# One decoding step of attention with an MLP: the query's copy released at a head's last maximum, and the closing weighted sums split anew

## The chip, the cores and the metric

The kernel runs on one core of a Trainium2 chip. The metric is the device time of one execution in microseconds (us). A core has five engines with queues of their own: TensorE (PE in a profile; its weight loads are PEld), VectorE (DVE), ScalarE (ACT), GpSimd (POOL) and SyncE (SP), which issues the transfers here. An engine takes its queue in order; between engines only semaphores order the work.

## The reference

One token x of 512 numbers is normalized and goes through grouped-query attention over a cache and through an MLP; both results are added to x.

```
xn = layernorm(x)                                  # 512
q  = (xn @ wq)                                     # 32 query heads of 128, 8 key/value heads
scores = q . k_cache * 128**-0.5                   # k_cache, v_cache: 8 heads x 65536 keys x 128
o  = softmax(scores) @ v_cache
y  = x + o.reshape(4096) @ wo + relu(xn @ w1) @ w2 # w1: 512 x 1792, w2: 1792 x 512
```

All is fp32. The two caches are 537 MB of the 561 MB that are read.

## The kernel before

**Opening.** SyncE loads wq in two transfers into the V buffer, then w1, then the first K part. GpSimd fills constants (`flip`, `ident`, `accq`, `qall`, `accy`). VectorE computes the layernorm (L214 to L245) and multiplies the 32 slices of wq by x's numbers in a hardware loop (L256 to L261). TensorE folds that into q (L264). VectorE then builds small constants: `blk` (L269), which TensorE needs for the normalized x (L284); `idg` (L282, L283); later `sel` (L326 to L328), `selb`, `selg` and `rowg` (L333). The MLP's first product (w1) and the relu end in `hs[:, :14]`, the 14 scales of w2's slices.

**Main loop.** Each of the 8 heads has 4 parts of 16384 keys; a step is one part. K and V of a part are 8 MB each. There is one K buffer and one V buffer, so SyncE issues V of step i when V's buffer is free and K of step i+1 when K's is. In a step TensorE makes scores (L380) from the query in `qcur`, VectorE transposes them (L436) and takes maxima (L445, L450), ScalarE exponentiates (L416), and TensorE sums over V (L398) into `acc_o`. At the end of a head VectorE scales and sums `masked` (L479, L484) and adds `kept` (L486).

**The query's copy.** GpSimd holds all queries in `qall` and copies the next head's into `qcur` (L411) when `f_out` is raised (waited for at L410). VectorE raises `f_out` at L484. The copy is made after the last head too, of an empty column.

**Closing sums.** 14 slices of w2 and 32 of wo remain, each 128 x 512 numbers (256 KB), each to be scaled by its column of `hs` and summed over partitions and slices. Arrived slices lie one behind the other in the old K buffer. They are loaded in pieces: w2 as 3, 4 and 7 slices and wo as 9, 7, 5, 4, 4, 1, 1 and 1 (the list `WO`). w2 and wo's first two wait for the K buffer (`k_free`), the rest for the V buffer (`v_free`). In a profile's table of transfers w1 and w2 are `w`. The slices are worked off in four ways:

- The first `FIRST` = 7, all w2: ScalarE scales in place (L500), GpSimd adds into `accy` (L501).
- The next 2 x `TURNS` = 32, in a hardware loop of 16 turns (L532): in each, ScalarE scales the even slice (L538) and TensorE sums it with ones into `acc_z` (L540), while VectorE multiplies the odd slice and adds it into `accy` (L543).
- wo's slices from there to `DIRECT` = 29: TensorE alone, the scale as weights, one slice per column group of `acc_z` (L547).
- The last three: TensorE into `acc_y` (L559).

VectorE folds `accy` and `acc_z` (L554), TensorE sums that into `acc_y` (L559), VectorE transposes it (L583) and SyncE stores 2 KB.

The loop's turns are handed out by GpSimd: for each piece that arrives it raises `go_dve` (L528) and `go_act` (L529) by the slices in it. These instructions stand behind the seven adds in GpSimd's queue:

```
for j in range(FIRST):
    begun = kv[:, j * D : (j + 1) * D]
    AC.op(lambda e: e.activation(begun, begun, AF.Copy, scale=hs[:, j : j + 1]), w2_in[j])
    GP.op(lambda e: e.tensor_add(accy, accy, begun), AC.mark, GP.mark)
...
    ge.wait_ge(*arrivals[at]).then_inc(go_dve, sum((j - FIRST) % 2 for j in js))
    ge.sem_inc(go_act, sum((j - FIRST) % 2 == 0 for j in js))
```

The scales of wo's slices come from VectorE: the reciprocal of the softmax sums (L490, L492, L497), the heads' outputs spread by TensorE (L506) and transposed (L510), and their product (L512). GpSimd hands out wo's slices only behind L512, and VectorE enters the loop only behind GpSimd's last add.

Of the kernel before, what the change touches and what calls it, by code (L numbers as in the profile page):

```python
# [11 lines left out]
AX = mybir.AxisListType  # L12
# [3 lines left out]
P = 128  # L16
# [4 lines left out]
G = HQ // HKV  # L21
CT = 4
# [7 lines left out]
NP = NCH  # L30
STEPS = HKV * NP
WIDE = 4
A = D // P
FB = DFF // P
R = HKV
SLICES = R * G
WO = [9, 7, 5, 4, 4, 1, 1, 1]
DIRECT = 29
LATE = 21 * D
TURNS = 16  # L40
FIRST = 7
EPS = 1e-5


# [26 lines left out]
def attention_and_mlp_kernel(  # L71
# [30 lines left out]
    te, ve, se, ge, sy = nc.tensor, nc.vector, nc.scalar, nc.gpsimd, nc.sync  # L102
# [9 lines left out]
    t1, t2 = place("t1", A * DFF), ks[:, : FB * D]  # L112
# [6 lines left out]
    x16, xc, sq, xn16 = (place(n, 32, rows=R * 2) for n in ("x16", "xc", "sq", "xn16"))  # L119
    xw, xn = place("xw", R, A), place("xn", A)  # L120
    rep, blk = (place(n, P, rows=R * 2) for n in ("rep", "blk"))
# [7 lines left out]
    ident, ones = place("ident", P), place("ones", P)  # L129
    sel, selb, selg = place("sel", WIDE, G), place("selb", WIDE), place("selg", G)  # L130
    rowg = place("rowg", P, rows=G)
    idg = place("idg", G + 1, rows=G)
    qall, qcur = place("qall", HKV + 1, G), place("qcur", 32)
    m, mc = place("m", G), place("mc", G)
    mg = place("mg", 1, rows=G)
# [15 lines left out]
    pr, pt, pz = pa[:, 0, :], pb[:, 0, :], pb[:, 1, :]  # L151
# [16 lines left out]
    def load_slices(name, dst, src, counts, at=0):  # L168
        marks = []
        for n in counts:  # L170
            cut = slice((at + len(marks)) * D, (at + len(marks) + n) * D)
            marks += [load(sy, f"{name}{at + len(marks)}", dst[:, cut], src[:, cut])] * n
        return marks
# [14 lines left out]
    def memset(flow, ap, value):  # L188
        return flow.op(lambda e: e.memset(ap, value))

    far_dve, far_act, far_pool = (e.mark_branch_hint_location() for e in (ve, se, ge))
    memset(GP, flip, 0.0)
    flat_free = GP.mark
    g0 = memset(GP, ident, 0.0)
# [9 lines left out]
    memset(GP, qall, 0.0)  # L204
    memset(GP, accy, 0.0)
    blank = GP.mark
    memset(DV, ones, 1.0)
    memset(DV, qcur, 0.0)
    memset(DV, pm, 0.0)


    half = R * 2
    DV.op(
        lambda e: e.tensor_copy(  # L214
            rep.rearrange("i (h j) -> i h j", j=half), ident[:half, :half].unsqueeze(1).to_broadcast([half, HKV, half])
# [40 lines left out]
    with nc.Fori(0, SLICES, engines=[ENG.DVE]) as t:  # L256
# [8 lines left out]


    spread_x = masked[:half].rearrange("i b d -> i (b d)")
    DV.op(
        lambda e: e.tensor_copy(  # L269
            blk.rearrange("i (j r) -> i j r", r=R), ident[:half, :half].unsqueeze(2).to_broadcast([half, half, R])  # L270
        )
    )
    blk_in = DV.mark
    DV.op(lambda e: e.reduce_sum(eighth, ident.rearrange("p (i r) -> p r i", r=R), axis=AX.X))
    DV.op(
        lambda e: e.tensor_mul(
# [2 lines left out]
        ),  # L279
    )  # L280
    x_spread = DV.mark
    DV.op(lambda e: e.memset(idg, 1.0))  # L282
    DV.op(lambda e: e.tensor_copy(idg[:, :G], ident[:G, :G]), DV.mark)  # L283
    xn_in = PE.op(lambda e: e.matmul(pz[:, :32], blk, xn16, start=True, stop=True), blk_in)  # L284
    DV.op(lambda e: e.tensor_copy(rows[:HKV], pr[:HKV]), q_in_rows)
    for g in range(G):
        PE.op(
# [1 line left out]
            DV.mark,  # L289
        )  # L290
    q_turned = PE.mark
    PE.op(lambda e: e.matmul(acc_z, ident[:half], spread_x, start=True, stop=False), x_spread)
    DV.op(
        lambda e: e.tensor_mul(
            xw, x_of.rearrange("p (r a) -> p r a", a=A), eighth.unsqueeze(2).to_broadcast([P, R, A])
        ),
        xn_in,
    )
    DV.op(lambda e: e.reduce_sum(xn, xw.rearrange("p r a -> p a r"), axis=AX.X), DV.mark)
    DV.op(  # L300
# [14 lines left out]
    for c in range(CT):  # L315
# [4 lines left out]
    mlp_in = PE.mark  # L320


    places = [ident[:, 32 * c : 32 * c + WIDE * G].rearrange("p (b g) -> p b g", g=G) for c in range(CT)]
    memset(DV, acc_o, 0.0)
    memset(DV, acc_y[:, :P], 0.0)
    DV.op(lambda e: e.tensor_add(sel, places[0], places[1]), made)  # L326
    DV.op(lambda e: e.tensor_add(sel, sel, places[2]), DV.mark)
    DV.op(lambda e: e.tensor_add(sel, sel, places[3]), DV.mark)  # L328
    s = DV.mark
    DV.op(lambda e: e.reduce_sum(selb, sel, axis=AX.X), s)  # L330
    DV.op(lambda e: e.reduce_sum(selg, sel.rearrange("p b g -> p g b"), axis=AX.X), s)
    DV.op(
        lambda e: e.tensor_copy(  # L333
            rowg.rearrange("g (i j) -> g i j", j=G), ident[:G, :G].unsqueeze(1).to_broadcast([G, P // G, G])
        )
    )
    DV.op(lambda e: e.transpose(turned, pm[:, : 32 * FB]), mlp_in)
    DV.op(
        lambda e: e.tensor_scalar_max(hs[:, :FB], turned.rearrange("p (j l) -> p j l", l=32)[:, :, 0], 0.0), DV.mark
# [19 lines left out]
    sy.dma_start(vs[:, :LATE], v_parts[STEPS - 1][:, :LATE]).then_inc(v_in, 16)  # L359
    sy.dma_start(vs[:, LATE:], v_parts[STEPS - 1][:, LATE:]).then_inc(v_late, 16)  # L360
    sy.wait_ge(k_free, 1)
    w2_in = load_slices("w2", t2, w2.rearrange("p j n -> p (j n)"), [3, FB // 2 - 3, FB // 2])
    wo_of = wo.rearrange("h (i r) g f -> (h i) (r g f)", r=R)
    near = [n for i, n in enumerate(WO) if FB + sum(WO[: i + 1]) <= SLICES]
    wo_in = load_slices("wo", wos, wo_of, near)
# [41 lines left out]
    with nc.Fori(0, HKV, engines=[ENG.DVE, ENG.Activation, ENG.Pool]) as h:  # L407
        fin_d, fin_s = finss[:, bass.ds(h * (DH + G), DH)], finss[:, bass.ds(h * (DH + G) + DH, G)]
        ve.lower_ap(fin_d), ve.lower_ap(fin_s)
        ge.wait_ge(f_out, 1).then_inc(f_out, -1)  # L410
        ge.tensor_copy(qcur[:, :G], qalls[:, bass.ds((h + 1) * G, G)]).then_inc(q_in, NP)  # L411

        for n in range(NP):
            se.wait_ge(s_bias, 1).then_inc(s_bias, -1)  # L414
            for g in range(G):
                i = se.activation(  # L416
                    wt[:, :, g], tr[:, :, g], AF.Exp, bias=bias[:, n, g : g + 1],
                    scale=scale, accum_out=part[:, n, g : g + 1],
                )
            i.then_inc(s_w, 1)  # L420
            if n:
                se.activation(
                    alpha[:, n : n + 1], bias[:, n - 1, G : G + 1], AF.Exp,
                    bias=bias[:, n, G : G + 1], scale=-1.0,
                ).then_inc(s_alpha, 1)
        se.wait_ge(s_diff, 1).then_inc(s_diff, -1)
        se.activation(
            fac.rearrange("p n g -> p (n g)"), diff.rearrange("p n g -> p (n g)"), AF.Exp
        ).then_inc(s_alpha, 1)

        for n in range(NP):
            for s in range(0, NT, 2):
                if s == NT - 2:

                    ve.wait_ge(s_tiles, NT // 2).then_inc(k_free, 1)
                i = ve.transpose(  # L436
                    tr[:, s * SUB : (s + 2) * SUB, :].rearrange("p b i -> p (b i)"),
                    (pa, pb)[s // 2 % 2].rearrange("p i k -> p (i k)"),
                )._wait_ge(s_tiles, s // 2 + 1)
                if s < 4:  # L440
                    i.then_inc(s_dve, 1)
            ve.sem_inc(s_tiles, -4)
            ve.drain()
            top = m if n == 0 else mc
            i = ve.reduce_max(top, tr[:, :, :G].rearrange("p b g -> p g b"), axis=AX.X)  # L445
            if n:
                ve.drain()
                i = ve.tensor_max(m, m, mc)  # L448
            i.then_inc(s_dve, 1)
            ve.reduce_max(mg, pm[:G, :P], axis=AX.X)._wait_ge(s_max, 1)  # L450
            ve.drain()
            ve.tensor_scalar(dg, idg, mg, -scale, op0=ALU.mult, op1=ALU.mult).then_inc(s_dve, 1)  # L452
            ve.tensor_copy(bias[:, n, :], pm[:, P : P + G + 1])._wait_ge(s_max, 2).then_inc(s_bias, 1)
            ve.sem_inc(s_max, -2)
            if n:
                ve.wait_ge(s_alpha, 1).then_inc(s_alpha, -1)
            if n == NP - 1:
                ve.drain()
                last = bias[:, NP - 1, :G].unsqueeze(1).to_broadcast([P, NP - 1, G])
                ve.tensor_sub(diff, last, bias[:, : NP - 1, :G]).then_inc(s_diff, 1)  # L460
                ve.scalar_tensor_tensor(
                    masked, acc, alpha[:, n : n + 1], selb.unsqueeze(2).to_broadcast([P, WIDE, DH]),
                    op0=ALU.mult, op1=ALU.mult,
                )
                ve.wait_ge(s_alpha, 1).then_inc(s_alpha, -1)
                ve.tensor_mul(part[:, : NP - 1, :], part[:, : NP - 1, :], fac)
                ve.drain()
                ve.reduce_sum(fin_s, part.rearrange("p n g -> p g n"), axis=AX.X).then_inc(sums_in, 1)
                ve.reduce_sum(kept, masked.rearrange("p b d -> p d b"), axis=AX.X)
            ve.wait_ge(s_o, 1).then_inc(v_free, 1)  # L470
            if n == 0:
                ve.tensor_copy(flat, acc_o)  # L472
            elif n < NP - 1:
                ve.scalar_tensor_tensor(  # L474
                    flat, flat, alpha[:, n : n + 1], acc_o, op0=ALU.mult, op1=ALU.add
                )
            else:
                ve.drain()
                ve.tensor_mul(  # L479
                    masked, acc_o.rearrange("p (b d) -> p b d", d=DH), selb.unsqueeze(2).to_broadcast([P, WIDE, DH])  # L480
                )
            ve.sem_inc(s_o, -1)
        ve.drain()
        ve.reduce_sum(fin_d, masked.rearrange("p b d -> p d b"), axis=AX.X).then_inc(f_out, 1)  # L484
        ve.drain()
        ve.tensor_add(fin_d, fin_d, kept).then_inc(fins_in, 1)  # L486

# [133 lines left out]
```

## Time and profile before

| what | value |
|---|---|
| median of 3 runs | 1312.58 us (1311.82 to 1313.63) |
| profiled execution | 1311.72 us |
| its span, first to last instruction | 1310.3 us |
| moved by DMA | 561.02 MB, mean 428 GB/s |
| busy: PE / PEld / DVE | 645.7 / 179.4 / 324.5 us |
| busy: ACT / POOL | 91.2 / 13.3 us |
| mean granted TensorE clock | 0.747 of full speed |

The span is what the trace shows; the execution's time is 1.4 us longer. Times in a trace count from the span's start. A row of the timeline gives start, duration, engine, line of the kernel, operation, output <- input, and in brackets how long the engine had been idle and what ended that; a "q" behind an engine's name (POOLq, PEq) is its sequencer, which handles waits and semaphores. An fp32 matmul shows as two passes. The granted clock is 0.5 or 1.0 of full speed at any moment.

### The profile page before, as it was taken

Reading aid. Unit: us, or ns where it says so; the run is one execution under the profiler, and the core shown is the slowest. Engines: PE = TensorE matmul, PEld = TensorE weight load, DVE = VectorE, ACT = ScalarE, POOL = GpSimd, SP = SyncE. Lnnn points to the kernel's source line nnn. Section 1 sums busy time; section 2 is a strip of 40 time slices with the busy share of each in tenths; the row PEclk is TensorE's granted clock in tenths of the full one; section 3 lists DMA queues with packets and bytes.
Section 4 is the critical chain, followed back from the end, with each engine's and each line's share of the span. In section 5 each row is a group of like instructions: output and inputs, shape, how many; then the busy total and the mean of one; then the engine's idle time right before and its main releaser. Section 6 shows DMA issues by size and latency. Waiting matters only on the chain. (4 is left out here: it accounts for less than half of the span.)

```text
span 1310.3 us, 11160 instructions
## 1 busy us (share of the span) xinstructions
PE 645.7 (49%) x4358; PEld 179.4 (14%) x4358; DVE 324.5 (25%) x471; ACT 91.2 (7%) x315; POOL 13.3 (1%) x26
## 2 busy tenths in 40 slices
PE   0453554554464455456345445535545544544555
PEld 0111111111111111111111111111111111111111
DVE  6711222211322222122221123222022222202225
ACT  0000000000000000000000000000000000000013
POOL 0000000000000000000000000000000000000002
PEclk9977767776776777786777677677677768767777
DMA  9999999999999999999999999999999999999996
GB/s 402 446 429 434 444 420 446 418 446 420 444 420 444 430 436 440 424 446 418 446 420 444 420 444 426 440 434 430 444 420 446 420 444 420 444 420 446 430 419 258
DMA packets 11554, 561.02 MB, mean 428 GB/s; under 512 B 1440, under 2 KB 1440, under 8 KB 1952
## 3 DMA queue, kind: packets, MB, share of 16 engines
q1 hardware_dynamic: 11520, 561.00, 99.1%
q8 instruction: 1, 0.02, 0.0%
q10 hardware_dynamic: 32, 0.00, 0.0%
q14 instruction: 1, 0.01, 0.0%
HBM read 560.99 MB, written 0.00 MB: 428 GB/s over the span
## 5 line engine op out<-in xcount | busy, mean ns | idle before, releaser
L398 PE MATMUL acc_o<-kv,wt 128*16 128x512 f32 x2048 | 293.6, 738 | 176.2 <-PEq L392 176.2
L380 PE MATMUL pa<-kv,qcur 128*32 128x512 f32 x1024 | 175.4, 818 | 316.7 <-PEq L375 316.7
L436 DVE STREAM_TRANSPOSE tr<-pa 128x1024 f32<-128x1024 f32 x64 | 80.0, 1250 | 408.4 <-PE pa L380 408.4
L416 ACT ACTIVATE wt<-tr,bias 128x128 f32<-128x128 f32 x128 | 64.2, 511 | 1180.5 <-ACTq L414 1180.5
L380 PE MATMUL pb<-kv,qcur 128*32 128x512 f32 x1024 | 136.6, 653 | 0.0
L398 PEld LDWEIGHTS acc_o<-kv,wt 128*16 128x16 f32 x2048 | 69.3, 113 | 373.8 <-issue 373.8
L380 PEld LDWEIGHTS pa<-kv,qcur 128*32 128x32 f32 x1024 | 39.1, 134 | 424.5 <-issue 414.4
L436 DVE STREAM_TRANSPOSE tr<-pb 128x1024 f32<-128x1024 f32 x64 | 80.0, 1250 | 46.9 <-PE pb L380 46.9
L474 DVE SCALAR_TENSOR_TENSOR acc<-acc,alpha,acc_o 128x512 f32<-128x512 f32 x16 | 12.0, 747 | 235.4 <-PE acc_o L398 235.4
L380 PEld LDWEIGHTS pb<-kv,qcur 128*32 128x32 f32 x1024 | 41.3, 130 | 105.4 <-issue 86.3
L385 PE MATMUL pm<-ident,m 128*4 128x128 f32 x32 | 9.8, 306 | 87.8 <-DVE m L448 67.2
L472 DVE COPY acc<-acc_o 128x512 f32<-128x512 f32 x8 | 5.5, 691 | 118.0 <-PE acc_o L398 118.0
L261 DVE SCALAR_TENSOR_TENSOR acc<-kv,xs,acc 128x512 f32<-128x512 f32 x32 | 24.0, 751 | 6.9 <-DVEq L260 6.9
L479 DVE TENSOR_TENSOR masked<-acc_o,selb 128x512 f32<-128x512 f32 x8 | 5.5, 692 | 78.5 <-PE acc_o L398 78.5
L386 PE MATMUL pm<-dg,ones 4*128 4x4 f32 x64 | 14.4, 293 | 21.4 <-DVE dg L452 21.4
L445 DVE TENSOR_REDUCE mc<-tr 128x4 f32<-128x512 f32 x24 | 24.1, 1006 | 1.8
L416 ACT ACTIVATION_READ_ACCUMULATOR wt<-tr,bias 128x1 f32 x128 | 23.9, 186 | 0.0
L540 PE MATMUL acc_z<-kv,ones 128*1 x32 | 15.5, 646 | 8.9 <-PEq L539 8.9
L385 PEld LDWEIGHTS pm<-ident,m 128*4 128x4 f32 x32 | 2.6, 81 | 116.8 <-DVE m L448 89.0
L264 PE MATMUL pa<-acc,mine 128*8 128x512 f32 x2 | 1.9, 1038 | 31.3 <-DVEq L262 31.3
L386 PEld LDWEIGHTS pm<-dg,ones 4*128 4x128 f32 x64 | 11.6, 225 | 28.6 <-DVE dg L452 28.6
L543 DVE SCALAR_TENSOR_TENSOR accy<-kv,hs,accy 128x512 f32<-128x512 f32 x16 | 12.0, 751 | 10.1 <-DVEq L542 10.1
(106 smaller groups left out, 167.8 us busy)
## 6 DMA issues: line engine op xcount, KB each, us to landing
kv<-wq SPq DMA_DIRECT2D x2, 4096.0 KB, 16.8
kv<-v SPq DMA_DIRECT2D x1, 5376.0 KB, 22.0
t<-w SPq DMA_DIRECT2D x1, 3584.0 KB, 29.5
kv<-v SPq DMA_DIRECT2D x1, 2816.0 KB, 28.3
kv<-wo SPq DMA_DIRECT2D x1, 2304.0 KB, 23.4
kv<-wo SPq DMA_DIRECT2D x2, 1024.0 KB, 19.0
kv<-w SPq DMA_DIRECT2D x1, 1792.0 KB, 18.4
kv<-wo SPq DMA_DIRECT2D x1, 1792.0 KB, 27.2
```

The source lines that it names most:

```text
L261: ve.scalar_tensor_tensor(accq, slice_t, x_t, accq, op0=ALU.mult, op1=ALU.add).then_inc(own, 1)
L380: i = te.matmul(tile_of[32 * c : 32 * c + 32, :], qcur, ks[:, at : at + TW], start=True, stop=True)
L385: te.transpose(pm[:G, :P], m, ident)._wait_ge(s_dve, 3).then_inc(s_max, 1)
L386: te.matmul(pm[:, P : P + G], ones[:G, :], dg[:, :G], start=True, stop=True)._wait_ge(s_dve, 4)
L398: mm = te.matmul(acc_o[32 * c : 32 * c + WIDE * G, :], wt[:, i * WIDE : (i + 1) * WIDE, :].rearrange("p b g -> p (b g)"), vs[:, i * 512 : ...
L416: i = se.activation(wt[:, :, g], tr[:, :, g], AF.Exp, bias=bias[:, n, g : g + 1], scale=scale, accum_out=part[:, n, g : g + 1],)
L436: i = ve.transpose(tr[:, s * SUB : (s + 2) * SUB, :].rearrange("p b i -> p (b i)"), (pa, pb)[s // 2 % 2].rearrange("p i k -> p (i k)"),)._ ...
L445: i = ve.reduce_max(top, tr[:, :, :G].rearrange("p b g -> p g b"), axis=AX.X)
L472: ve.tensor_copy(flat, acc_o)
L474: ve.scalar_tensor_tensor(flat, flat, alpha[:, n : n + 1], acc_o, op0=ALU.mult, op1=ALU.add)
L540: te.matmul(acc_z[:1], ones[:, 0:1], even, start=False, stop=False)
L543: ve.scalar_tensor_tensor(accy, odd, scale_o, accy, op0=ALU.mult, op1=ALU.add).then_inc(own, 1)
```

## The change

Four things change.

1. `f_out` is raised by the maximum of a head's last part (L450, `n == NP - 1`), not by L484.
2. `FIRST` is 4 and `TURNS` 18: four slices of w2 go to GpSimd's adds, 36 slices to the loop. w2 is loaded in two pieces, of 4 and 10 slices, and wo's fourth and fifth piece are 5 and 3 slices, not 4 and 4. Three slices are left for L547.
3. As one of the four column groups of `acc_z` has no slice in L547 any more, the matmul that starts `acc_z` (L292) writes 96 rows, and VectorE clears the other 32.
4. `blk`, `rowg`, `idg` and `sel` are built by GpSimd in the opening, not by VectorE.

```
-WO = [9, 7, 5, 4, 4, 1, 1, 1]
+WO = [9, 7, 5, 5, 3, 1, 1, 1]
-TURNS = 16
-FIRST = 7
+TURNS = 18
+FIRST = 4
...
     memset(GP, accy, 0.0)
     blank = GP.mark
+    GP.op(
+        lambda e: e.tensor_copy(
+            blk.rearrange("i (j r) -> i j r", r=R), ident[:half, :half].unsqueeze(2).to_broadcast([half, half, R])
+        ),
+        made,
+    )
...
+    memset(GP, idg, 1.0)
+    GP.op(lambda e: e.tensor_copy(idg[:, :G], ident[:G, :G]), GP.mark)
...
+    GP.op(lambda e: e.tensor_add(sel, places[0], places[1]))
+    GP.op(lambda e: e.tensor_add(sel, sel, places[2]), GP.mark)
+    GP.op(lambda e: e.tensor_add(sel, sel, places[3]), GP.mark)
+    shapes = GP.mark
...
-    xn_in = PE.op(lambda e: e.matmul(pz[:, :32], blk, xn16, start=True, stop=True), blk_in)
+    xn_in = PE.op(lambda e: e.matmul(pz[:, :32], blk, xn16, start=True, stop=True), shapes)
...
-    PE.op(lambda e: e.matmul(acc_z, ident[:half], spread_x, start=True, stop=False), x_spread)
+    PE.op(lambda e: e.matmul(acc_z[:96], ident[:half, :96], spread_x, start=True, stop=False), x_spread)
...
+    memset(DV, acc_z[96:], 0.0)
...
-    w2_in = load_slices("w2", t2, w2.rearrange("p j n -> p (j n)"), [3, FB // 2 - 3, FB // 2])
+    w2_in = load_slices("w2", t2, w2.rearrange("p j n -> p (j n)"), [FIRST, FB - FIRST])
...
-            ve.reduce_max(mg, pm[:G, :P], axis=AX.X)._wait_ge(s_max, 1)
+            i = ve.reduce_max(mg, pm[:G, :P], axis=AX.X)._wait_ge(s_max, 1)
+            if n == NP - 1:
+                i.then_inc(f_out, 1)
...
-        ve.reduce_sum(fin_d, masked.rearrange("p b d -> p d b"), axis=AX.X).then_inc(f_out, 1)
+        ve.reduce_sum(fin_d, masked.rearrange("p b d -> p d b"), axis=AX.X)
```

Where instructions moved, the queues are shown below; a row gives the line (of its own version), the operation, output <- input, the output's size, and in brackets the semaphores waited for. On GpSimd, in the opening, before:

```order
L196 AFFINE_SELECT ident<-ident 128x128
L189 MEMSET acc 128x512
L189 MEMSET qall 128x36
L189 MEMSET accy 128x512
L371 COPY qcur<-qall 128x4 [waits wq0,wq16,dve]
```

and now:

```order
L189 MEMSET accy 128x512
L209 COPY blk<-ident 16x128 [waits pool]
L215 COPY rowg<-ident 4x128
L189 MEMSET idg 4x5
L220 COPY idg<-ident 4x4 [waits pool]
L222 TENSOR_TENSOR sel<-ident 128x16
L223 TENSOR_TENSOR sel<-sel,ident 128x16 [waits pool]
L224 TENSOR_TENSOR sel<-sel,ident 128x16 [waits pool]
L372 COPY qcur<-qall 128x4 [waits wq0,wq16,dve]
```

Seven small operations stand between GpSimd's fills and its wait for wq. Further down in GpSimd's queue, from the main loop to the adds, the order is as it was, with four adds in place of seven. In TensorE's queue, from the heads' outputs to the last projections, stood before:

```order
L506 MATMUL pb<-fins,selg 4x256 [waits fins_in]
L506 MATMUL pb<-fins,selg 4x256 x3
L532 UNCONDITIONAL_BRANCH
L540 ISA [waits go_pe]
L540 MATMUL acc_z<-kv,ones 1x512
L532 REGISTER_ALU
L532 COMPARE_AND_BRANCH
L547 MATMUL acc_z<-kv,hs 1x512 [waits dve,wo25]
L547 MATMUL acc_z<-kv,hs 1x512 x3
L559 MATMUL acc_y<-kv,hs 1x128 [waits wo29]
```

and stands now:

```order
L509 MATMUL pb<-fins,selg 4x256 [waits fins_in]
L509 MATMUL pb<-fins,selg 4x256 x3
L535 UNCONDITIONAL_BRANCH
L543 ISA [waits go_pe]
L543 MATMUL acc_z<-kv,ones 1x512
L535 REGISTER_ALU
L535 COMPARE_AND_BRANCH
L550 MATMUL acc_z<-kv,hs 1x512 [waits dve,wo26]
L550 MATMUL acc_z<-kv,hs 1x512 x2
L562 MATMUL acc_y<-kv,hs 1x128 [waits wo29]
```

One matmul of four is gone behind the loop, and the wait there is for wo's slice 26, not 25; the loop's body is the same and turns 18 times.

More of the change, by code (lines that the diff above doesn't have):

```diff
@@ L191, in attention_and_mlp_kernel @@
     far_dve, far_act, far_pool = (e.mark_branch_hint_location() for e in (ve, se, ge))
+    half = R * 2
     memset(GP, flip, 0.0)
@@ L206, in attention_and_mlp_kernel @@
     blank = GP.mark
+    GP.op(
[4 more added lines that the diff above has]
+    )
+    GP.op(
+        lambda e: e.tensor_copy(
+            rowg.rearrange("g (i j) -> g i j", j=G), ident[:G, :G].unsqueeze(1).to_broadcast([G, P // G, G])
+        )
+    )
+    memset(GP, idg, 1.0)
+    GP.op(lambda e: e.tensor_copy(idg[:, :G], ident[:G, :G]), GP.mark)
+    places = [ident[:, 32 * c : 32 * c + WIDE * G].rearrange("p (b g) -> p b g", g=G) for c in range(CT)]
+    GP.op(lambda e: e.tensor_add(sel, places[0], places[1]))
+    GP.op(lambda e: e.tensor_add(sel, sel, places[2]), GP.mark)
+    GP.op(lambda e: e.tensor_add(sel, sel, places[3]), GP.mark)
+    shapes = GP.mark
     memset(DV, ones, 1.0)
@@ L209, in attention_and_mlp_kernel @@
     memset(DV, pm, 0.0)
-    half = R * 2
     DV.op(
@@ L267, in attention_and_mlp_kernel @@
     spread_x = masked[:half].rearrange("i b d -> i (b d)")
[L268 to L273, printed above, removed]
     DV.op(lambda e: e.reduce_sum(eighth, ident.rearrange("p (i r) -> p r i", r=R), axis=AX.X))
@@ L281, in attention_and_mlp_kernel @@
     x_spread = DV.mark
-    DV.op(lambda e: e.memset(idg, 1.0))
-    DV.op(lambda e: e.tensor_copy(idg[:, :G], ident[:G, :G]), DV.mark)
-    xn_in = PE.op(lambda e: e.matmul(pz[:, :32], blk, xn16, start=True, stop=True), blk_in)
+    xn_in = PE.op(lambda e: e.matmul(pz[:, :32], blk, xn16, start=True, stop=True), shapes)
     DV.op(lambda e: e.tensor_copy(rows[:HKV], pr[:HKV]), q_in_rows)
@@ L296, in attention_and_mlp_kernel @@
         ),
-        xn_in,
+        xn_in, x_spread,
     )
@@ L320, in attention_and_mlp_kernel @@
     mlp_in = PE.mark
-    places = [ident[:, 32 * c : 32 * c + WIDE * G].rearrange("p (b g) -> p b g", g=G) for c in range(CT)]
     memset(DV, acc_o, 0.0)
+    memset(DV, acc_z[96:], 0.0)
     memset(DV, acc_y[:, :P], 0.0)
[L326 to L336, printed above, removed]
+    DV.op(lambda e: e.reduce_sum(selb, sel, axis=AX.X), shapes)
+    DV.op(lambda e: e.reduce_sum(selg, sel.rearrange("p b g -> p g b"), axis=AX.X))
     DV.op(lambda e: e.transpose(turned, pm[:, : 32 * FB]), mlp_in)
```

## The prediction

> **What bounds the kernel now.** I read the view of engines and DMA in chosen stretches first. Of each row the last two columns count here: the mean busy share of the 16 DMA engines, and GB/s.
>
> ```profile
> 80.00:1260.00 1180.00, 591.44 (x4070) 165.50 (x4066) 252.87 (x346) 68.38 (x270) 1.30 (x7) 0.73 1.00 433
> 1260.00:1295.00 35.00, 17.90 (x97) 4.17 (x90) 14.59 (x26) 13.66 (x27) 9.03 (x8) 0.71 0.99 419
> ...
> 1297.00:1299.00 2.00, 2.00 (x6) 0.38 (x5) 1.51 (x3) 2.00 (x4) 0.00 (x0) 1.00 0.38 141
> 1299.00:1300.00 1.00, 1.00 (x4) 0.20 (x3) 0.81 (x2) 0.12 (x1) 0.00 (x0) 1.00 0.02 6
> ```
>
> The DMA engines are full from the opening to about 1297 us, while TensorE (the first column) is busy half the time: until then the caches' bytes set the pace, and nothing that an engine does earlier can shorten it. But the span ends at 1310.3. Some 11 us at the end belong to the engines, and the chain that ended last says to which:
>
> ```profile
> 1289.36 14.20 PE acc_z L540 x29
> ...
> 1305.82 0.70 DVE rows L554
> 1306.56 0.74 PE acc_y L559 x16
> 1307.32 0.41 DVE yt L583
> ```
>
> The closing loop on TensorE (L540) begins at 1289.36 and runs without a break. Behind it come the fold (L554), the last projections (L559), the transpose and the store, 4.5 us in all from 1305.82. So the question is why L540 begins so late. The timeline, by engine:
>
> ```profile
> 1263.75 0.28 DVE L450 TENSOR_REDUCE mg<-pm 4x1 f32<-4x128 f32 x1 [0.36 <-PE pm L385]
> ...
> 1273.21 1.95 ACT L500 ACTIVATE kv<-kv,hs 128x512 f32<-128x512 f32 x3 [4.92 <-DMA kv<-w]
> ...
> 1277.84 1.03 DVE L484 TENSOR_REDUCE fins<-masked 128x512 f32 x1
> ...
> 1279.12 0.19 POOL L411 COPY qcur<-qall 128x4 f32 x1 [150.34 <-POOLq L410]
> 1279.49 9.70 POOL L501 TENSOR_TENSOR accy<-accy,kv 128x512 f32<-128x512 f32 x7 [0.18 <-issue]
> ...
> 1288.33 0.72 ACT L538 ACTIVATE kv<-kv,hs  x1 [10.09 <-POOLq L529]
> ```
>
> GpSimd waits at L410 for VectorE's last sum (L484) to copy a query that nobody uses any more, then adds seven slices, 1.39 us each (9.70/7), and only then, in its queue, comes to L528 and L529, which hand the arrived slices to ScalarE and VectorE. ScalarE idles 10.09 us for that (its first turn starts 0.4 us after GpSimd's seventh add has begun), and TensorE waits for ScalarE. Were the slices there?
>
> ```profile
> 1261.61 0.43 SPq L165 DMA_DIRECT2D kv<-w  x1
> ...
> 1262.08 0.91 SPq L165 DMA_DIRECT2D kv<-wo  x2
> ...
> 1276.96 2.70 SPq L165 DMA_DIRECT2D kv<-wo  x6
> ...
> kv<-wo SPq DMA_DIRECT2D x1, 2304.0 KB, 23.4
> ...
> kv<-w SPq DMA_DIRECT2D x1, 1792.0 KB, 18.4
> kv<-wo SPq DMA_DIRECT2D x1, 1792.0 KB, 27.2
> kv<-wo SPq DMA_DIRECT2D x1, 1280.0 KB, 15.9
> ...
> kv<-wo SPq DMA_DIRECT2D x3, 256.0 KB, 20.4
> ```
>
> Issue plus time to landing: the last w2 transfer at 1261.61 + 18.4 = 1280.0, wo's first at 1285.5, its second at 1262.5 + 27.2 = 1289.7, its third at 1292.9, and the last slice at 1299.7 (the middle one of the three single slices is issued about 1278.75 and lands 1299.1; a slice takes 0.63 us at 419 GB/s). So at 1280.0 there was work for the loop, which began 8 us later.
>
> **The change, part by part.**
>
> *The release and the four adds.* The query is now released by the last head's L450, at 1264.0, so GpSimd is free when data come. The first w2 transfer holds four slices, one more: 1273.2 + 0.6 = 1273.8. ScalarE delivers its first at 1274.5 (1.95/3 = 0.65 each), GpSimd adds four until 1274.5 + 4 x 1.39 = 1280.1. It reaches the hand-over with its fourth add under way at 1278.8, so the ten remaining w2 slices, whose one transfer ends with the same byte as before, release the loop at 1280.0. With the 0.4 us to ScalarE and the 1.03 us from there to TensorE (1288.33 to 1289.36), L540 starts at 1281.5 instead of 1289.36: 7.9 us earlier. What is late next on TensorE is L506, below; it ends at the same time.
>
> *Two turns more.* The loop takes 36 slices, 18 turns. A turn is two passes on TensorE; the weight loads show the time from one to the next, gap plus load:
>
> ```profile
> 1291.03 0.13 PEld L540 LDWEIGHTS acc_z<-kv,ones 128*1 128x1 f32 x1 [0.73 <-issue]
> ...
> 1298.25 0.08 PEld L540 LDWEIGHTS acc_z<-kv,ones 128*1 128x1 f32 x1 [0.34 <-issue]
> ...
> 1289.20:1292.60 3.40, 3.24 (x4) 0.47 (x5) 2.28 (x4) 3.40 (x6) 0.00 (x0) 0.50 1.00 419
> 1292.60:1296.00 3.40, 3.40 (x9) 0.67 (x8) 2.89 (x4) 3.40 (x6) 0.00 (x0) 1.00 0.99 408
> ```
>
> 0.86 us at half clock, 0.42 to 0.43 at full clock (third column from the right: 0.50, then 1.00). Four passes more cost 4 x 0.43 = 1.7 us. The matmul dropped from L547, one of four that run beside each other on column groups, is worth nothing, or up to 0.1 us. Net: L554 starts at 1305.8 - 7.9 + 1.7 = 1299.6.
>
> *The clock.* Before, TensorE was at half clock for the loop's first 3.3 us only. I take the same now; the loop is fed without gaps (below), and L506 already runs just ahead of it. [...]
>
> *VectorE, and GpSimd's adds beside it.* VectorE must finish the head and the weights (L512) before its own half of the loop:
>
> ```profile
> 44.97 0.17 DVE L294 TENSOR_TENSOR xw<-pb,eighth 128x32 f32<-128x32 f32 x1
> ...
> 1278.96 0.29 DVE L486 TENSOR_TENSOR fins<-fins,kept 128x128 f32 x1
> 1279.31 1.10 PE L506 MATMUL pb<-fins,selg 128*4 128x256 f32 x8 [2.12 <-DVE fins L486]
> 1279.61 1.20 DVE L492 TENSOR_TENSOR per<-total,mine 128x32 f32<-128x32 f32 x1
> 1281.42 0.80 DVE L512 TENSOR_TENSOR hs<-tr,inv 128x32 f32<-128x32 f32 x1
> ...
> L543 DVE SCALAR_TENSOR_TENSOR accy<-kv,hs,accy x16: 750/751/753, 1289.8 to 1303.6; 128x512 f32<-128x512 f32 x16
> ```
>
> L492 and L512 took 1.0 and 0.6 us longer than L294 on the same shape, each until a GpSimd add ended. With the adds at 1274.5 to 1280.1 that cost moves: L486 (due at 1278.96, under the fourth add) may be held until 1280.1 and L506 run to 1281.5, while L492 and L512 run free. The one gives 1.1 us away, the other up to 1.6 back, so the weights are ready at 1281.1 to 1282.2, as before or a little sooner. VectorE's 18 turns at 13.8/15 = 0.92 us then end at 1282.4 + 17 x 0.92 + 0.75 = 1298.8, under TensorE's 1299.5. It is the next bound, 0.7 us away.
>
> *Arrivals inside the loop.* wo's groups of 9, 7, 5, 5 and 3 slices are first used in turns 5, 10, 13, 16 and behind the loop. TensorE reaches these at about 1287.5, 1291.8, 1294.4 and 1296.9; the data are there at 1285.5, 1289.7, 1292.9, and, for the second group of five, one slice behind the old 1024 KB one, at 1296.0. No wait, though the last margin is under 1 us.
>
> *The moved set-up.* GpSimd now makes blk, rowg, idg and sel (seven small operations; its own small copy L411 takes 0.19, so some 2 us) behind its fills, and VectorE drops its versions and clears 32 rows of acc_z. What hides either sign:
>
> ```profile
> 5.20 1.03 DVE L214 COPY rep<-ident 16x128 f32<-16x128 f32 x1
> ...
> 13.43 0.75 DVE L261 SCALAR_TENSOR_TENSOR acc<-kv,xs,acc 128x512 f32<-128x512 f32 x1 [2.00 <-DVEq L260]
> ...
> 42.85 0.34 SPq L350 DMA_DIRECT2D kv<-v  x1
> ...
> 40.00:60.00 20.00, 9.76 (x34) 2.55 (x38) 14.13 (x26) 0.00 (x0) 1.08 (x1) 1.00 1.08 466
> ```
>
> VectorE's opening may be held by the new GpSimd copies (L214 already took 1.03 us beside the fills), but its first L261 waits 2.00 us for wq, so up to 2 us vanish there; behind it the first V transfer is queued at 42.85 into DMA engines that are full through 60 us. 0 us in the sum, 0 to +0.5 in the range.
>
> *The release in the other seven heads.* It comes earlier there too and buys nothing: TensorE waits for K, not for the query.
>
> ```profile
> 199.99 0.19 POOL L411 COPY qcur<-qall 128x4 f32 x1 [152.85 <-POOLq L410]
> ...
> 207.23 3.56 PE L380 MATMUL pa<-kv,qcur 128*32 128x512 f32 x16 [9.52 <-PEq L375]
> ```
>
> **Sum.** -7.9 + 1.7 = -6.2 us; the span goes from 1310.3 to 1304.1. The profiled execution took 1311.72 us, 1.4 more than its span, so 1305.5; the median of the runs, 1312.58, lies 0.9 above that execution, so 1306.4 for the median. I say 1306.5.
>
> **The rivals.** A measurement of this kernel can tell about 0.2% (2.6 us) from no change.
>
> [...]
> 2. *Another bound takes over.* If TensorE is faster than I think (the clock opens at once), VectorE's 1298.9, or the last slice at 1299.7 with the 3.7 us that follow L554, sets the end at about 1303.4: -6.9, 1305.7. This is also the floor for any start of the loop.
> 3. *Most is given back, no change to be seen.* The loop now runs 1 to 2 us behind the arrivals instead of 8; if it starves at wo's groups, TensorE idles and drops to half clock again. [...] Against: at half clock it also consumes more slowly, so the data get ahead of it.
> 4. *Slower: TensorE stays at half clock through the loop.* 38 passes at 0.86 us are 32.7: L554 at 1281.5 + 32.7 = 1314.2, 8.4 later than before, 1321. [...] For it: the loop of before, too, began at 0.50, and the one of now follows the arrivals more closely. Against it: once fed, TensorE left half clock after 3.3 us.
>
> **How the numbers follow.** The sum 0.70, second window 0.15, other bound 0.08, given back 0.05, slower 0.02. The predicted time is the likeliest case's. The range covers rivals 1 and 2 with half a microsecond for the runs' spread (1311.82 to 1313.63 before): 1305.2 to 1308.8. Faster by over 0.2%: the first three cases, 0.93; within: 0.05; slower: 0.02.
>
> **What would show it.** In the profile of the changed kernel: the last L411 copy near 1264; four adds ending near 1280.1; ScalarE's first loop turn at 1280.4 and TensorE's at 1281.5; L486 or its successors stretched instead of L492 and L512; L554 at 1299.6, 4.5 us ahead of the end; DMA ending at 1299.7 as before. The prediction is wrong if the loop starts later than 1283, if TensorE's clock falls back to 0.50 inside it, or if the DMA engines end at another time.

## The result, and the profile after

The changed kernel takes 1305.49 us (median of 6 runs, 1304.81 to 1306.49) against 1313.16 us of the kernel before (6 runs, 1311.82 to 1314.50): ratio 0.9942, 95% interval 0.9929 to 0.9954, or 7.7 us less by the medians. Forecast were 1306.5 us and 6.1 us less. The profiled execution took 1306.49 us with a span of 1305.2.

The timeline after, of the closing part (line numbers are those of the changed kernel: L412 was L411, L487 was L484, L503 and L504 were L500 and L501, L541 was L538, L543 was L540, L557 was L554):

```profile
1265.06 0.19 POOL L412 COPY qcur<-qall 128x4 f32 x1 [154.03 <-POOLq L411]
...
1273.56 2.56 ACT L503 ACTIVATE kv<-kv,hs 128x512 f32<-128x512 f32 x4 [4.08 <-DMA kv<-w]
1274.36 5.52 POOL L504 TENSOR_TENSOR accy<-accy,kv 128x512 f32<-128x512 f32 x4 [9.12 <-ACT kv L503]
...
1279.24 1.03 DVE L487 TENSOR_REDUCE fins<-masked 128x512 f32 x1
1280.09 3.44 ACT L541 ACTIVATE kv<-kv,hs  x5 [3.97 <-ACTq L540]
1280.34 0.29 DVE L489 TENSOR_TENSOR fins<-fins,kept 128x128 f32 x1
...
1280.69 1.10 PE L509 MATMUL pb<-fins,selg 128*4 128x256 f32 x8 [2.10 <-DVE fins L489]
...
1281.59 15.12 PE L543 MATMUL acc_z<-kv,ones 128*1 x32
...
1282.42 0.19 DVE L515 TENSOR_TENSOR hs<-tr,inv 128x32 f32<-128x32 f32 x1
...
1296.04 1.39 ACT L541 ACTIVATE kv<-kv,hs  x2 [1.03 <-ACTq L540]
1297.07 1.45 PE L543 MATMUL acc_z<-kv,ones 128*1 x3 [0.35 <-PEq L542]
...
1299.91 0.69 DVE L557 TENSOR_TENSOR rows<-accy,acc_z 128x512 f32<-128x512 f32 x1 [0.84 <-PE acc_z L550]
```

The idle times in brackets tell the story. GpSimd is free from 1265.3 and now waits 9.12 us for data; the data no longer wait for GpSimd. Its four adds are over at 1279.88. TensorE's loop starts at 1281.59 and takes 36 passes in a row but for one gap: at 1297.07 it waited 0.35 us, because ScalarE had waited 1.03 us at L540 for the piece of wo that holds the slices of turns 16 and 17.

The clock in the loop (stretch and its length, busy time of five engines, granted clock, DMA share, GB/s):

```profile
1281.59:1283.00 1.41, 1.41 (x6) 0.23 (x2) 0.67 (x3) 1.41 (x3) 0.00 (x0) 0.50 1.04 444
1283.00:1284.00 1.00, 1.00 (x2) 0.13 (x1) 0.83 (x2) 0.53 (x1) 0.00 (x0) 0.52 0.87 369
1284.00:1285.00 1.00, 1.00 (x4) 0.25 (x3) 0.85 (x2) 0.00 (x0) 0.00 (x0) 1.00 0.99 420
```

Full speed came 2.4 us after the loop's start, against 3.2 before (1289.36 to 1292.6).

### The profile page after: what moved, and what is told of

Read it like the earlier page. It is cut to its first block, busy times and chain, and to the rows that moved or that the text cites. A ratio compares the mean times of both kernels' runs of the same rounds, so it can differ in the third digit from the quotient of the medians.

```text
span 1305.2 us, 11192 instructions
## 1 busy us (share of the span) xinstructions
PE 647.6 (50%) x4360; PEld 180.5 (14%) x4360; DVE 324.1 (25%) x467; ACT 90.8 (7%) x314; POOL 10.9 (1%) x30
## 5 line engine op out<-in xcount | busy, mean ns | idle before, releaser
L543 PE MATMUL acc_z<-kv,ones 128*1 x36 | 17.0, 627 | 0.4 <-PEq L542 0.4
L388 PE MATMUL pm<-dg,rowg 4*128 4x1 f32 x64 | 14.5, 293 | 0.0
```

Source lines behind the costliest of these rows:

```text
L388: te.matmul(pm[:, P + G : P + G + 1], rowg, dg[:, G : G + 1], start=True, stop=True).then_inc(s_max, 1)
L543: te.matmul(acc_z[:1], ones[:, 0:1], even, start=False, stop=False)
```

## The experiments

Ratios are to the kernel before, run on the same chip. The changed kernel's own ratio was 0.9942 in the result above and, once more on another chip, 0.9937.

**Release alone, split alone.** The change has two parts that could each bring the loop forward. First the early release by itself:

```
# the kernel before, with only:
-            ve.reduce_max(mg, pm[:G, :P], axis=AX.X)._wait_ge(s_max, 1)
+            i = ve.reduce_max(mg, pm[:G, :P], axis=AX.X)._wait_ge(s_max, 1)
+            if n == NP - 1:
+                i.then_inc(f_out, 1)
...
-        ve.reduce_sum(fin_d, masked...).then_inc(f_out, 1)
+        ve.reduce_sum(fin_d, masked...)
```

> The kernel before with the earlier release alone (f_out at a head's last maximum); seven adds, 16 turns, the set-up on VectorE and 455 TensorE instructions stay. Theory A (the closing loop's start and length decide): GpSimd adds from 1274.0, seven times 1.39 us, reaches the hand-over under its last add at 1282.4; TensorE's loop starts at about 1283.9 instead of 1289.4, 16 turns as before: 5.5 us less than the kernel before, about 1307.7. Theory B (part of the gain is that the two instruction fetches of 8 and 16 KB, seen in the queue table of before and absent after, no longer hold two DMA engines): the fetches should be there again, and the gain the same 5.5 us, with the last of the 16 DMA engines again 1.4 us late.

Measured: 1307.47 us, ratio 0.9955 (0.9942 to 0.9969), 5.8 us less by the medians. Then the split by itself:

```
# the kernel before, with only:
-WO = [9, 7, 5, 4, 4, 1, 1, 1]        +WO = [9, 7, 5, 5, 3, 1, 1, 1]
-TURNS = 16                           +TURNS = 18
-FIRST = 7                            +FIRST = 4
# w2 in 4 and 10 slices; acc_z started on 96 rows and cleared on 32
```

> The kernel before with the new split alone: four adds, 18 turns, w2 in 4 and 10 slices, wo 5 and 3, three slices in TensorE's column groups; the late release and the set-up on VectorE stay; 451 TensorE instructions. Theory A: GpSimd adds from 1279.5, the fourth add begins at 1283.7, TensorE's loop starts at 1285.1 and takes two turns more (1.7 us): 2.5 us less than before, about 1310.7. Theory B: no instruction fetch in the run, so 1.0 to 1.5 us less again: about 1309.5.

Measured: 1310.23 us, ratio 0.9978 (0.9968 to 0.9988), 3.0 us less. The rows of the two timelines, first of the release alone, then of the split alone (their lines L503, L502 are GpSimd's adds, L542, L541 TensorE's loop):

```profile
1274.15 9.77 POOL L503 TENSOR_TENSOR accy<-accy,kv 128x512 f32<-128x512 f32 x7 [9.44 <-ACT kv L502]
...
1284.10 15.28 PE L542 MATMUL acc_z<-kv,ones 128*1 x29 [3.10 <-PEq L541]
```

```profile
1280.04 5.49 POOL L502 TENSOR_TENSOR accy<-accy,kv 128x512 f32<-128x512 f32 x4 [0.18 <-issue]
...
1285.70 16.41 PE L541 MATMUL acc_z<-kv,ones 128*1 x33 [4.75 <-PEq L540]
```

With the release alone the adds begin when data come but there are seven; with the split alone there are four, but they begin at the head's end. In both the loop starts within 0.6 us of the computed place (1283.9 and 1285.1), and the gains are near those computed (5.5 and 2.5 us). The two parts overlap: 5.8 and 3.0 us alone, 7.7 together.

The fit of the release alone is in part luck. Its loop stayed at half clock for 5.4 us, not 3.2: TensorE's weight loads there, 0.85 us apart, come 0.43 us apart only from 1289.77 on.

```profile
1289.17 0.13 PEld L542 LDWEIGHTS acc_z<-kv,ones 128*1 128x1 f32 x1 [0.72 <-issue]
1289.77 0.09 PEld L542 LDWEIGHTS acc_z<-kv,ones 128*1 128x1 f32 x1 [0.47 <-issue]
...
1290.20 0.08 PEld L542 LDWEIGHTS acc_z<-kv,ones 128*1 128x1 f32 x1 [0.34 <-issue]
```

So from the loop's start to the fold (1301.63) it took 17.5 us, 1.1 more than the 16.5 of the kernel before. Something else made that up: the start of the kernel before, from which the 5.5 us were counted, was an early one, as the second profile of that kernel shows below.

**TensorE's 451 instructions.** The page after lacks two rows that the page before has:

```profile
q8 instruction: 1, 0.02, 0.0%
...
q14 instruction: 1, 0.01, 0.0%
```

These are transfers of instructions, of 16 KB (q8) and 8 KB (q14), in the run. If they slowed the caches' stream, the shorter program itself would be worth something. The changed kernel was brought back to 455 instructions by a matmul that never executes:

```
     with nc.body("again", valid_engines=hinted):
+        te.matmul(pt[:1, :P], ones[:, 0:1], ones, start=True, stop=True)
```

> The changed kernel with one matmul (four TensorE instructions) put into the block that is never executed, so that TensorE has 455 instructions as before. Theory A: no difference from the changed kernel, 1305.5 within 0.5 us. Theory B: the two instruction fetches are back in the queue table and the time is 1.0 to 1.5 us longer, about 1306.7.

Measured: 1304.83 us, ratio 0.9939 (0.9925 to 0.9953): not slower, and no transfer of instructions came back. So the count as such does not bring them. The other way round, the kernel before was shortened to 451; it leaves out one slice of wo's sum:

```
# the kernel before, acc_z started on 96 rows, and:
-    for j in range(end, gathered):
+    for j in range(end + 1, gathered):
```

> The kernel before with 451 TensorE instructions: one of the four matmuls behind the loop is left out, and with it one slice of wo's sum (acc_z is started on 96 rows, as in the changed kernel). Theory A: no difference from the kernel before, 1313.2 within 0.5 us. Theory B: no instruction fetches in the queue table, and 1.0 to 1.5 us less, about 1312.

Measured: 1312.69 us, ratio 0.9996 (0.9986 to 1.0005). The 16 KB transfer was gone, the 8 KB one was not, and the time was the same within the interval. That interval alone still allows a price of up to 1.8 us. But the release alone had both transfers in its table and gained 5.8 us, and this run and the change without the set-up (below) have the same transfers, the 8 KB one alone: their ratios, 0.9996 and 0.9944, are 0.0052 or 6.8 us apart. So at least most of the gain is not from there.

**The set-up.** Alone it would show whether GpSimd's seven small operations, or VectorE's shorter program, matter.

```
# the kernel before, with only blk, rowg, idg and sel built by GpSimd in the opening
```

> The kernel before with the set-up moved to GpSimd and nothing else. Theory A: the kernel before, 1313.3 within 0.6 us; the first V transfer is issued within 0.5 us of 42.85. Theory C: 0.6 to 1.5 us less. The queue table should show the 16 KB fetch (TensorE as long as before) and not the 8 KB one (VectorE shorter).

Measured: 1314.21 us, ratio 1.0004 (0.9995 to 1.0013): no difference that can be told. The first V transfer was issued at 42.56. And the change without it:

```
# the changed kernel, with blk, rowg, idg and sel back on VectorE
```

> The changed kernel with the set-up back on VectorE: early release and new split, nothing else. Theory A (the closing loop alone): the changed kernel's time, 1305.3 within 0.6 us. Theory C (the set-up's move has a share of the gain, directly or by the 8 KB instruction fetch, which goes with VectorE's longer program): 0.6 to 1.5 us slower than the changed kernel.

Measured: 1305.93 us, ratio 0.9944 (0.9931 to 0.9958), as the change's 0.9942. The queue tables of the two, set-up alone and change without set-up:

```profile
q8 instruction: 1, 0.02, 0.0%
```

```profile
q14 instruction: 1, 0.01, 0.0%
```

So release and split make the gain. The interval of the set-up alone reaches from 0.7 us less to 1.7 us more; a share of the set-up within that is not excluded.

**The kernel before once more.**

```
# the kernel before, unchanged
```

> The kernel before, profiled once more, to see what moves from one execution to the next. If its spread comes from the clock in the last head (TensorE's last sums over V end sooner or later, and VectorE's last sum, GpSimd's copy and the closing loop follow it): the copy L411 at 1279 to 1281 and the span moves with it one to one. If the spread lies elsewhere: the copy within 0.3 us of 1279.1. Both instruction fetches again in the queue table.

Measured: 1313.47 us, span 1312.1 against 1310.3 in the first profile. Its timeline:

```profile
1280.70 0.19 POOL L411 COPY qcur<-qall 128x4 f32 x1 [150.50 <-POOLq L410]
...
1290.95 14.28 PE L540 MATMUL acc_z<-kv,ones 128*1 x29 [8.95 <-PEq L539]
...
1307.49 0.69 DVE L554 TENSOR_TENSOR rows<-accy,acc_z 128x512 f32<-128x512 f32 x1 [1.53 <-PE acc_z L547]
```

The copy came 1.58 us later than in the first profile, the loop 1.59, the fold 1.67: one to one. Of this, 1.1 us was there when TensorE took up the last K part (1253.27 instead of 1252.17, by the timelines; it waits for K's landing there), 0.3 came from a slower start of its scores in that part, and 0.2 from its last sums over V (L398, 9.46 us instead of 9.30).

**What ends the new loop.** After the change TensorE waits before turn 16. Finer pieces should release that turn earlier:

```
-WO = [9, 7, 5, 5, 3, 1, 1, 1]
+WO = [9, 7, 5, 3, 2, 3, 1, 1, 1]
```

> The changed kernel with wo's fourth piece of 5 slices loaded as 3 and 2, so that the loop's turn 16 need not wait for slices that turn 17 uses. If that piece's landing sets the end (TensorE waited 0.35 us before turn 16 in the trace after, and ScalarE started that turn 0.4 us after the landing): the fold starts 0.5 to 1.0 us earlier and the time is 1304.4 to 1305. If the last slice's landing or VectorE's turns set it: no change from the changed kernel, within 0.4 us.

Measured: 1304.70 us, ratio 0.9934 (0.9920 to 0.9947). This looked like a gain, so it was run beside the changed kernel on one chip, with a coarser cut as the opposite dose (`WO = [9, 7, 5, 8, 1, 1, 1]`):

> The changed kernel once more, on the same chip as the two that follow: 1305.3 within 0.6 us, no instruction fetch in the queue table. Theory D (the landing of wo's last piece of the loop sets the end): the fold L557 starts 4.3 us after that piece has landed.

> The changed kernel with wo's piece of 5 slices as 3 and 2, once more. Theory D: 0.5 to 1.0 us less than the changed kernel beside it. If the end is set by the last slice: within 0.3 us of it.

> The changed kernel with wo's pieces of 5 and 3 slices loaded as one of 8, so that the last turns of the loop become free 3 slices (1.9 us) later; everything else as it is. Theory D: the fold starts 1.9 us later, the time is about 1307.2. If the loop's start and TensorE's passes alone set the end: the wait is shorter than 0.5 us and the time 1305.3 to 1305.8.

Measured: the changed kernel 1305.04 us (0.9937, interval 0.9924 to 0.9951), the finer cut 1305.15 (0.9940, 0.9927 to 0.9954), the coarser 1306.20 (0.9946, 0.9932 to 0.9960). Both times that theory D gave were missed: 0.5 to 1.0 us less for the finer cut, about 1307.2 for the coarser. Timelines of the changed kernel and of the coarser cut, ScalarE's turns 16 and 17 and the fold:

```profile
1295.15 1.39 ACT L541 ACTIVATE kv<-kv,hs  x2 [1.04 <-ACTq L540]
...
1299.03 0.69 DVE L557 TENSOR_TENSOR rows<-accy,acc_z 128x512 f32<-128x512 f32 x1 [1.44 <-PE acc_z L550]
```

```profile
1297.57 1.39 ACT L541 ACTIVATE kv<-kv,hs  x2 [2.84 <-ACTq L540]
1298.60 1.45 PE L543 MATMUL acc_z<-kv,ones 128*1 x3 [2.16 <-PEq L542]
...
1301.45 0.69 DVE L557 TENSOR_TENSOR rows<-accy,acc_z 128x512 f32<-128x512 f32 x1 [1.44 <-PE acc_z L550]
```

From ScalarE's turn 16 to the fold it is 3.88 us in both (and 3.87 in the first profile after): the fold does hang on that piece's landing. But the time moved by 1.2 us only where the fold moved by 2.4, and not at all for the finer cut, whose fold came 0.34 us earlier (1298.69). What took the rest in the profiled executions is the final store; the row is that of the coarser cut:

```profile
y<-yt SPq DMA_DIRECT2D x1, 2.0 KB, 1.4
```

It landed 1.4 us after its issue with the coarser cut, after 2.7 with the changed kernel and 2.9 with the finer cut. Why it differs so is open. The finer cut is no resolvable gain; no version better than the changed kernel was found.

## Why the prediction was right, point by point

- *Where the time lay.* Right. The 11 us behind the caches' transfers held the gain, and the closing loop's late start was its cause. The rivals "given back" and "slower" did not come: the granted clock was 1.00 from 2.4 us after the loop's start to the fold.
- *The start of the loop.* 1281.5 was forecast and 1281.59 measured. ScalarE's first turn came at 1280.09 (forecast 1280.4); with the 1.03 us from there it allowed a start at 1281.12. L509 came last, as forecast, but for another reason: the forecast had the adds hold VectorE's instruction ahead of it, whereas here the head's last sum itself came 1.4 us later than before (1279.24, not 1277.84), and the adds were over at 1279.88. That the place agrees to 0.1 us is luck. The forecast mechanism stands in the second profile of the changed kernel. There the last sum began at 1276.79, and L489 was held until the adds ended at 1278.99; with L509 running to 1280.31 and ScalarE's first turn at 1279.20, the loop began at 1280.24:

```profile
1277.90 1.24 DVE L489 TENSOR_TENSOR fins<-fins,kept 128x128 f32 x1
...
1280.24 4.97 PE L543 MATMUL acc_z<-kv,ones 128*1 x10
...
1285.77 7.03 PE L543 MATMUL acc_z<-kv,ones 128*1 x16 [0.56 <-PEq L542]
...
1293.13 2.73 PE L543 MATMUL acc_z<-kv,ones 128*1 x6 [0.33 <-PEq L542]
...
1296.18 1.45 PE L543 MATMUL acc_z<-kv,ones 128*1 x3 [0.32 <-PEq L542]
```

- *The gain from it, -7.9 us.* This is the term that was mis-sized; it took the first profile's own start, 1289.36, as the kernel's usual one. Of the three later profiles of the old order one, the set-up alone, starts its loop as early (1289.29); in the other two (the kernel before again, and the one shortened to 451) the last head ended later and the seven adds with it. The shortened one makes the fair pair with the profile after, for its head's last sum begins at 1279.29 (1279.24 after):

```profile
1279.29 1.02 DVE L485 TENSOR_REDUCE fins<-masked 128x512 f32 x1
...
1290.82 14.30 PE L541 MATMUL acc_z<-kv,ones 128*1 x29 [8.97 <-PEq L540]
...
1307.38 0.69 DVE L555 TENSOR_TENSOR rows<-accy,acc_z 128x512 f32<-128x512 f32 x1 [1.55 <-PE acc_z L548]
```

  There the loop starts 9.2 us later than after the change and the fold 7.5 us later, close to the measured difference of 7.7. In the old order the loop starts 11.5 us behind that last sum (1277.84 to 1289.36, 1279.29 to 1290.82); in the new one 2.35 (1279.24 to 1281.59), or 3.45 where the adds hold L489 (1276.79 to 1280.24). Adding the same 0.9 us from profile to median on both sides was thus wrong. After, the profiled execution was the slowest of its six. Before, the offset was most likely the late head; only profiled executions show where the head ended, so this stays an inference. The same 0.9 us is in the "floor" of 1305.7 us of the rival "another bound takes over"; the median came out 0.2 us below it.
- *Two turns, +1.7 us.* From the loop's start to the fold it was 16.46 and 16.56 us before (1289.36, 1290.82) and 18.32 after: +1.8, right, though composed otherwise. The shorter start at half clock (2.4 us, not 3.2) gave about 0.4 back, and the wait in the next point took it.
- *Arrivals: "no wait".* Wrong. I set the landing against TensorE's use and left out the hand-over that the same text prices at 0.4 + 1.03 us from landing to TensorE. With it the piece that lands at 1296.0 in the forecast is usable at 1297.4, behind TensorE's 1296.9. The fold came at 1299.91, forecast 1299.6. In the second profile, whose loop began 1.35 us earlier, TensorE waited three times (0.56, 0.33 and 0.32 us, rows above), and the fold came only 0.88 us earlier: the arrivals are the next bound, and not VectorE, which the prediction names.
- *The clock.* The 0.15 for a second window of half clock, at +1.7 us, the upper end of the range with it and the 0.05 for "given back" use a term that no run shows. What the runs showed is half clock at the loop's start, of differing length: 2.4 us with the whole change, 5.4 with the release alone and 4.2 with the split alone; the 5.4 made the way to the fold 1.1 us longer. By the spacing of its weight loads (0.85 us at half clock, 0.43 at full), the loop began with 1.1 to 2.5 us at half clock in the seven profiles with both parts, where it follows L509 without a gap, and with 3.2 to 5.4 us in the six others, where TensorE had idled 3.1 to 9.0 us. That is in line with the reason the forecast gives for a start at half clock no longer than before, L506 (now L509) just ahead of the loop; no run tried it by itself.
- *VectorE and the adds.* L489 was not stretched (0.29 us): the adds ended at 1279.88, just ahead of it. So the forecast sign of a stretched instruction was missing there; it came in the second profile (1.24 us, above). In the release alone, where seven adds run on, the same instruction and two of its followers took 0.60, 1.02 and 0.80 us, against 0.29, 0.22 and 0.19 after:

```profile
1279.23 0.60 DVE L488 TENSOR_TENSOR fins<-fins,kept 128x128 f32 x1
...
1280.14 1.02 DVE L494 TENSOR_TENSOR per<-total,mine 128x32 f32<-128x32 f32 x1
...
1281.77 0.80 DVE L514 TENSOR_TENSOR hs<-tr,inv 128x32 f32<-128x32 f32 x1
```

- *Set-up and the other heads' release.* The set-up was forecast at zero and showed nothing (ratio 1.0004 alone). The other heads' release was not run by itself; that it is worth nothing stays argued.

## What to carry to other kernels

When transfers fill the run, look only at what comes behind the last of them, and there at what a late engine's queue holds back although its data have landed: a hand-over behind an unneeded wait and a few slow adds cost nearly 8 us here. Price a hand-over on both sides, from landing to the engine that uses the data, before calling an arrival hidden. And before building a sum on one execution's start times, ask which earlier event moves them: the same kernel's loop began 1.6 us later in its next profile.

## What the runs showed of the hardware

- Instructions were fetched by transfers in the run, one of 16 KB and one of 8 KB in the first profile of the kernel before and none in that of the changed one; small changes of the program decided which. The 16 KB one was in the queue tables of the four profiles whose programs execute all of 455 TensorE instructions, and in none with fewer; 455 with four in a block that is never executed did not bring it. The 8 KB one was there where VectorE kept the set-up, and nowhere else. No price was measured for either; the intervals leave room for up to 1.8 us.
- A 2 KB store took 1.4 to 3.3 us from issue to landing (1.4 with the coarser cut, 3.3 in the first profile after), a spread as large as what the finer and the coarser cut were to show.
- The same loop began with 1.1 to 5.4 us at half clock: 1.1 to 2.5 where L509 (1.10 to 1.12 us) ran up to its start, 3.2 to 5.4 where TensorE had idled 3.1 to 9.0 us.
- VectorE operations were longer beside GpSimd's adds: the same sum (L489) took 0.29 us without and 1.24 us with them (second profile of the changed kernel), until the adds were over.
